# A limit of three loads in flight on SyncE in the listed opening phase of a retention and feed-forward kernel

## The chip, the cores and the metric

The kernel runs on one core of a Trainium2 chip. The metric is the device time of one execution in microseconds (us), lower is better. A difference of about 0.5% (4.4 us) is what the measurement can tell from no change.

## What is computed

Attention without softmax but with a decay by distance ("retention") over 4 batches, 8 heads, 576 positions and a head size of 64, then two feed-forward layers over the 2304 tokens of width 512:

```python
scores = scale * np.matmul(q, k.transpose(0, 1, 3, 2))
ret = scores * Dmat[None]            # Dmat[h, i, j] = gamma[h] ** (i - j), 0 above the diagonal
x = np.matmul(ret, v)                # reshaped to 2304 x 512
h = x @ w_in                         # 512 -> 2048
g = np.where(h >= 1, h, np.where(h <= -1, 0.0, (h + 1) ** 2 / 4))
x = g @ w_out                        # 2048 -> 512
out = ((x @ w_a) * (x @ w_b)) @ w_out2      # 512 -> 1536 -> 512
```

The weights are stored in double precision and are converted in the kernel.

## The kernel before

The tokens are cut into 18 chunks of 128 and 6 blocks of 384. For a chunk the retention needs a `u` tile of 1 MB (queries, keys, keys by row and values), which two loads of 512 KB bring (`load_chunk`, line 460; chunks 4 and 5 lie in tiles named `uw`). A weight tile is loaded as `raw`, 512 KB of doubles (`load_raw`, line 184), and then turned into a high and a low float32 part by ScalarE, VectorE and GpSimd.

The opening phase, some 113 us long, is written out by hand: `ORDER` (line 41) is a list of tokens, each a letter and a number, and every engine receives its instructions in the order of that list. The letters that matter here: `u` loads a chunk, `r` a raw weight tile, `c` a part of the constants; `S` multiplies queries by keys, `V` scales the values on GpSimd, `P` makes the chunk's output on TensorE (tiles `po`); `X`, `C`, `O` bring it to the tile `x`; `A`, `B`, `F` or `f`, `H`, `W` are the five steps of a weight tile's conversion (`A` on ScalarE waits for the raw tile's landing); `L` is a product of the first feed-forward layer (tile `ph`), `T`, `U`, `G`, `J` its activation, `Z` a product of the second (`acc`); `K` is filler work on TensorE (`idle`). All loads of this phase stand on SyncE's queue (SP), in the order of the list, and SP issues nothing else in it. `BANKS` gives the PSUM bank of every `S`, `P` and `L`; the list `planned` holds what is left of it, so it is empty from the last such token (`L12`, near the end of the list) on.

The framework gives each DMA one of eight landing semaphores in turn (`DMAHW0` to `DMAHW7`). A DMA that takes one over waits for the landing of the one that held it, so up to eight DMAs are in flight. After the listed phase the order is by loops and a scheduler; the change does not reach there.

Of the kernel before, what the change touches and what calls it, by code (L numbers as in the profile page):

```python
# [10 lines left out]
SYNC = mybir.DependencyInfo(mybir.DependencyClass.Sync, mybir.DependencyReason.DATA)  # L11
# [23 lines left out]
PACE = 1.2  # L35
MID = 288
CHUNKS = 4
SPARE, INTER_FIRST = (4, 5), 6
Q0, K0, R0, V0 = 0, 512, 0, 512

# [79 lines left out]
def retention_ffn_kernel(  # L120
# [12 lines left out]
    nc = tc.nc  # L133
    B, H, S, D = shape
    DM = H * D
# [14 lines left out]
    planned, ps = [int(n) for n in BANKS], []  # L150
# [26 lines left out]
    raw_pools, raw_turn, raw_every = [rpool], [0], [5]  # L177
    side = [nc.sync]

    def load_raw(src):  # L180
        r = raw_pools[-1] if raw_turn[0] % raw_every[0] == raw_every[0] - 1 else rpool
        raw_turn[0] += 1
        raw = r.tile([P, 512], I64, tag="raw", name="raw")
        side[0].dma_start(raw.rearrange("p (c f) -> p c f", f=src.shape[-1]), src)
        return raw

    def begin(raw, t=None):
# [63 lines left out]
    class Raws:  # L251
# [6 lines left out]
        def fetch_to(self, n):  # L258
            while self.begun < min(n, len(self.sources)):
                self.tiles[self.begun] = load_raw(self.sources[self.begun])  # L260
                self.begun += 1
# [139 lines left out]
    loads = []  # L401
# [18 lines left out]
    apool = att.enter_context(tc.tile_pool(name="att", bufs=1))  # L420
    upool = att.enter_context(tc.tile_pool(name="unit", bufs=CHUNKS))
    a2 = att.enter_context(tc.tile_pool(name="att2", bufs=2))
# [28 lines left out]
    def load_chunk(c):  # L451
        if c < NCH:
            if c in SPARE:
                two = [wpool.tile([P, 2, 512], F32R, tag="w", name="uw") for _ in range(2)]
                units[c] = [t.bitcast(F32).rearrange("p a c -> p (a c)") for t in two]
            else:
                t = upool.tile([P, 4 * DM], F32, tag="u", name="u")
                units[c] = [t[:, :2 * DM], t[:, 2 * DM:]]
            for part, t in enumerate(units[c]):
                nc.sync.dma_start(t, qkv[c, :, 2 * DM * part:2 * DM * part + 2 * DM])  # L460

    def prepare(c):

# [138 lines left out]
    def load_next(limit):  # L602

        while loaded[0] < min(limit, NCH):
            load_chunk(loaded[0])
            loaded[0] += 1
# [13 lines left out]
    def output_next():  # L620

        c = done[0]
        load_next(c + CHUNKS)
        given = output(c)
# [426 lines left out]
    def needed(step):  # L1051
# [1 line left out]

    half, parts, chunk, gen = {}, {}, {}, {}
    in_order = {
        "c": lambda k: nc.sync.dma_start(
            *((t[:, early:first] if k else t[:, :early]) for t in (con, const))
        ),
        "u": load_chunk, "r": lambda k: raws1.fetch_to(k + 1),
        "S": score, "V": prepare, "P": lambda c: chunk.update({c: evacuate(c, *output(c))}),  # L1060
        "X": lambda c: next(chunk[c]), "C": lambda c: next(chunk[c]), "O": lambda c: next(chunk[c]),
# [39 lines left out]
    for s, step in enumerate(steps[:last_by_hand]):  # L1101
        if s < by_order:
            continue
        i, b, f, first, last = step
# [49 lines left out]
    for s, step in enumerate(steps):  # L1154
        if s < last_by_hand:
            continue
        i, b, f, first, last = step
# [61 lines left out]
    for n in range(NSB):  # L1219
# [3 lines left out]
        for p in range(NF2 // 2):  # L1223
            for w in range(2):
# [11 lines left out]
                if quad:  # L1236
# [5 lines left out]
                    else:  # L1242
                        act2(other, quad)
                        f = 2 * quad.at[1]
# [73 lines left out]
```

## Time and profile before

| | |
|---|---|
| median of 3 runs | 874.16 us (873.89 to 878.53) |
| the profiled execution, its own time | 874.88 us |
| its span, first to last instruction | 873.0 us |
| TensorE matmul (PE) busy | 862.5 us, 99% |
| VectorE (DVE) busy | 577.4 us, 66% |
| ScalarE (ACT) busy | 446.5 us, 51% |
| GpSimd (POOL) busy | 81.1 us, 9% |
| DMA, mean over the span | 273 GB/s |
| DMA packets by queue | q1, loads and stores of SP: 196.87 MB; q0, of POOL: 40.37 MB; q8, instructions: 0.82 MB |

The profile is one execution. A row of the timeline tells start, duration, engine, line, operation, the tile written and the tiles read, how many instructions were merged, and in brackets how long the engine had been idle before and what ended that; "issue" there means that nothing the profile shows ended it. All products stand on line 157, a helper, so the tile's name tells them apart. The granted clock is the share of TensorE's full clock that the chip granted.

### The profile page before, as it was taken

The numbers are of one execution on the slowest core, as the hardware profiler recorded it, in microseconds if no ns is written. First come the engines' busy times: TensorE is split into PE (matmuls) and PEld (weight loads), VectorE is DVE, ScalarE is ACT, GpSimd is POOL, SyncE is SP. The second block draws the span as 40 slices with busy tenths as digits, with TensorE's granted clock in tenths as the row PEclk, the third lists the DMA queues.
The fourth block names the chain that finished last, engine by engine and source line by source line (L and its number), as shares of the span: only waits on it lengthen the run. The fifth ranks groups of instructions, "written<-read, shape, count | busy, mean of one in ns | idle before, by whom it ended". The sixth has DMA issues, their size and how long they took to land.

```text
span 873.0 us, 16378 instructions
## 1 busy us (share of the span) xinstructions
PE 862.5 (99%) x6308; PEld 847.7 (97%) x6308; DVE 577.4 (66%) x1088; ACT 446.5 (51%) x899; POOL 81.1 (9%) x124
## 2 busy tenths in 40 slices
PE   8899999999999999999999999999999999999998
PEld 6799999999999999999999999999999999999998
DVE  5787556576777789777779858752347575246465
ACT  4556355575766677666567546442233353333253
POOL 2313233110010011011001000000000000000000
PEclk9999999999999999999999999999999999999999
DMA  9997581648679889899889998879547589847583
GB/s 337 356 337 255 204 279 58 263 149 315 241 258 329 309 291 322 329 352 331 286 302 323 404 410 263 257 245 338 174 145 245 187 276 413 324 146 245 185 288 151
DMA packets 81373, 238.31 MB, mean 273 GB/s; under 512 B 8424, under 2 KB 35304, under 8 KB 78992
## 3 DMA queue, kind: packets, MB, share of 16 engines
q1 hardware_dynamic: 71616, 196.87, 63.2%
q0 software_dynamic: 9664, 40.37, 13.4%
q8 instruction: 50, 0.82, 0.4%
q14 instruction: 27, 0.22, 0.1%
q10 hardware_dynamic: 16, 0.02, 0.0%
HBM read 175.89 MB, written 61.34 MB: 272 GB/s over the span
## 4 chain that ended last, share of the span: by engine, by line
PE 99%; issue 1%; DVE 0%; ACT 0%
PE acc L157 35%; PE ph L157 23%; PE qx L157 17%; PE qy L157 9%; PE late L157 4%; PE qz L157 4%; PE po L157 4%; PE s L157 2%; PE idle L157 1%; PE wacc L157 0%; DVE keep L849 0%; DVE warm L1001 0%; ACT ost L976 0%
## 5 line engine op out<-in xcount | busy, mean ns | idle before, releaser
L157 PE MATMUL acc<-g,w 128*128 128x384 f32 x1296 | 249.0, 334 | 0.0
L157 PEld LDWEIGHTS acc<-g,w 128*128 128x128 f32 x1296 | 226.5, 188 | 0.4
L157 PE MATMUL ph<-x,w 128*128 128x384 f32 x1152 | 220.9, 336 | 0.0
L157 PEld LDWEIGHTS ph<-x,w 128*128 128x128 f32 x1152 | 201.6, 188 | 0.8 <-issue 0.2
L157 PE MATMUL qx<-tx,w 128*128 128x384 f32 x864 | 164.7, 334 | 0.0
L157 PEld LDWEIGHTS qx<-tx,w 128*128 128x128 f32 x864 | 151.1, 188 | 0.0
L793 ACT COPY keep<-qx 128x384 f32<-128x384 f32 x126 | 59.6, 480 | 141.3 <-PE qx L157 133.5
L661 ACT ACTIVATE t<-ph 128x384 f32<-128x384 f32 x96 | 47.1, 490 | 79.3 <-PE ph L157 75.1
L664 DVE SCALAR_TENSOR_TENSOR t<-t,ph 128x384 f32<-128x384 f32 x96 | 52.8, 551 | 51.9 <-ACT t L662 51.5
L157 PE MATMUL qy<-tx,w 128*128 128x384 f32 x432 | 86.3, 334 | 0.0
L157 PE MATMUL acc<-sp,w 128*128 128x384 f32 x432 | 77.5, 334 | 0.0
L157 PEld LDWEIGHTS qy<-tx,w 128*128 128x128 f32 x432 | 75.9, 188 | 0.0
L157 PEld LDWEIGHTS acc<-sp,w 128*128 128x128 f32 x432 | 75.1, 188 | 0.0
L669 ACT CAST g<-t 128x384 fp32r<-128x384 f32 x96 | 49.0, 510 | 40.7 <-DVE t L664 34.8
L671 DVE TENSOR_TENSOR g<-t,g 128x384 fp32r<-128x384 f32 x96 | 53.5, 557 | 20.8 <-ACT g L669 20.5
L886 DVE TENSOR_TENSOR sp<-gb,sp 128x768 fp32r<-128x768 f32 x42 | 40.1, 956 | 21.3 <-ACT sp L885 21.0
L662 ACT ACTIVATE t<-t 128x384 f32<-128x384 f32 x96 | 50.5, 526 | 2.7
L885 ACT CAST sp<-gb 128x768 fp32r<-128x768 f32 x42 | 35.1, 837 | 32.3 <-PE acc L157 18.8
L196 ACT ACTIVATE raw<-raw 128x512 int32<-128x512 uint32 x68 | 45.6, 671 | 2.7 <-DMA raw<-in_moe_w_out 2.7
L828 DVE TENSOR_TENSOR keep<-keep 128x384 f32<-128x384 f32 x36 | 20.0, 557 | 40.4 <-ACT keep L793 40.4
L157 PE MATMUL qz<-tx,w 128*128 128x384 f32 x216 | 43.4, 334 | 0.0
L815 DVE TENSOR_TENSOR keep<-qz,keep 128x384 f32<-128x384 f32 x36 | 20.0, 556 | 32.1 <-PE qz L157 27.7
(113 smaller groups left out, 944.9 us busy)
## 6 DMA issues: line engine op xcount, KB each, us to landing
w<-q SPq DMA_DIRECT2D x126, 512.0 KB, 5.3
q<-q SPq DMA_DIRECT2D x42, 512.0 KB, 7.1
w<-o SPq DMA_DIRECT2D x42, 512.0 KB, 5.1
x<-xd SPq DMA_DIRECT2D x12, 1536.0 KB, 8.6
u<-in_qkv SPq DMA_DIRECT2D x32, 512.0 KB, 8.3
raw<-in_moe_w_out POOLq DMA_DIRECT2D x18, 512.0 KB, 6.5
yin<-y SPq DMA_DIRECT2D x48, 192.0 KB, 4.3
xd<-x POOLq DMA_DIRECT2D x5, 1536.0 KB, 8.7
```

The lines of the kernel that those rows point to most:

```text
L157: return nc.tensor.matmul(o, l, r, start=start, stop=stop, skip_group_check=goes_on)
L196: nc.scalar.activation(r, low, AF.Copy, scale=2.0 ** -29)
L661: nc.scalar.activation(t, ph[:, :TB], AF.Relu, bias=0.5, scale=0.5)
L662: nc.scalar.activation(t, t, AF.Square)
L664: nc.vector.scalar_tensor_tensor(out=t, in0=t, scalar=1.0, in1=ph[:, :TB], op0=ALU.min, op1=ALU.max)
L669: hi = nc.scalar.copy(g[:, 0, :], t)
L671: anchor[:] = [hi, nc.vector.tensor_sub(g[:, 1, :], t, g[:, 0, :].bitcast(F32))]
L793: kept_by[0] = nc.scalar.copy(t, o[:, :HT])
L815: anchor[:] = [kept_by[0], nc.vector.tensor_add(self.c11, z[:, :HT], self.c11)]
L828: nc.vector.tensor_add(self.c22, self.c22, self.s5)
L885: nc.scalar.copy(t[:, 0], b)
L886: nc.vector.tensor_sub(t[:, 1], b, t[:, 0].bitcast(F32))
```

## The change

A constant `AHEAD = 3` and a function `load` are added. The loads of the phase go through it, and while `planned` is not empty each one gets a dependency on the landing of the third last.

```diff
+AHEAD = 3
...
+    sent = []
+
+    def load(to, of):
+        ins = side[0].dma_start(to, of)
+        if planned and len(sent) >= AHEAD:
+            tc.add_manual_dep(ins.ins, sent[-AHEAD].ins.name, SYNC, reason="loads in flight")
+        sent.append(ins)
+
     def load_raw(src):
...
-        side[0].dma_start(raw.rearrange("p (c f) -> p c f", f=src.shape[-1]), src)
+        load(raw.rearrange("p (c f) -> p c f", f=src.shape[-1]), src)
...
             for part, t in enumerate(units[c]):
-                nc.sync.dma_start(t, qkv[c, :, 2 * DM * part:2 * DM * part + 2 * DM])
+                load(t, qkv[c, :, 2 * DM * part:2 * DM * part + 2 * DM])
...
-        "c": lambda k: nc.sync.dma_start(
+        "c": lambda k: load(
```

Nothing changes its place on any engine; what changes is what the loads on SP wait for. Its queue from the second load of weights to chunk 5, before (`raw_330` and `raw_332` are raw weight tiles 1 and 2, `u_339` is chunk 3, the `uw` tiles are chunks 4 and 5; in brackets the semaphores waited for):

```order
L184 DMA raw_330<-in_moe_w_out 128x512 [waits DMAHW2_49]
L184 DMA raw_332<-in_moe_w_in 128x4x128 [waits DMAHW3_49]
L460 DMA u_339<-in_qkv 128x1024 [waits DMAHW4_49]
L460 DMA u_339<-in_qkv 128x1024 [waits DMAHW5_49]
L460 DMA uw_345<-in_qkv 128x1024 [waits DMAHW6_49]
L460 DMA uw_346<-in_qkv 128x1024 [waits DMAHW7_49]
L1056 DMA con_171<-in_const 128x192 [waits DMAHW0_49]
L460 DMA uw_485<-in_qkv 128x1024 [waits DMAHW1_49]
L460 DMA uw_486<-in_qkv 128x1024 [waits DMAHW2_49]
```

The same rows of SP now:

```order
L186 DMA raw_330<-in_moe_w_out 128x512 [waits DMAHW7_49,DMAHW2_49]
L186 DMA raw_332<-in_moe_w_in 128x4x128 [waits DMAHW0_49]
L186 DMA u_339<-in_qkv 128x1024 [waits DMAHW1_49]
L186 DMA u_339<-in_qkv 128x1024 [waits DMAHW2_49]
L186 DMA uw_345<-in_qkv 128x1024 [waits DMAHW3_49]
L186 DMA uw_346<-in_qkv 128x1024 [waits DMAHW4_49]
L186 DMA con_171<-in_const 128x192 [waits DMAHW5_49]
L186 DMA uw_485<-in_qkv 128x1024 [waits DMAHW6_49]
L186 DMA uw_486<-in_qkv 128x1024 [waits DMAHW7_49]
```

Each waits for the semaphore three places back in the turn of eight instead of its own one eight places back; the small load of constants counts as one of the three.

The end of the limit on SP, before (`u_1518` is chunk 14, `u_1602` chunk 15, `u_1835` chunk 16):

```order
L460 DMA u_1518<-in_qkv 128x1024 [waits DMAHW0_49,PE_49]
L460 DMA u_1518<-in_qkv 128x1024 [waits DMAHW1_49]
L460 DMA u_1602<-in_qkv 128x1024 [waits DMAHW2_49,PE_49,Pool_49]
L460 DMA u_1602<-in_qkv 128x1024 [waits DMAHW3_49]
L184 DMA raw_1748<-in_moe_w_in 128x4x128 [waits DMAHW4_49,DVE_49]
```

And now:

```order
L186 DMA u_1518<-in_qkv 128x1024 [waits DMAHW5_49,PE_49]
L186 DMA u_1518<-in_qkv 128x1024 [waits DMAHW6_49]
L186 DMA u_1602<-in_qkv 128x1024 [waits PE_49,Pool_49]
L186 DMA u_1602<-in_qkv 128x1024
L186 DMA raw_1748<-in_moe_w_in 128x4x128 [waits DVE_49]
```

From chunk 15 on no load waits for the third last one.

## Rows read from the trace of the kernel before

**Rows 1.** Busy time by stretch: us (instructions); last columns clock, DMA share, GB/s.

```profile
core 0: us, PE busy (x) PEld busy (x) DVE busy (x) ACT busy (x) POOL busy (x), PEclk, DMA share, GB/s
32.00:34.00 2.00, 2.00 (x21) 1.88 (x18) 1.45 (x4) 0.66 (x2) 0.00 (x0) 0.50 1.07 404
36.00:38.00 2.00, 2.00 (x51) 1.76 (x48) 1.14 (x4) 1.36 (x3) 1.78 (x3) 1.00 0.70 241
```

**Rows 2.** Chain of waits, 14 to 46 us: start, duration, what.

```profile
16.07 1.00 issue
...
21.56 0.57 PE s L157 x9
22.13 1.35 issue
...
26.39 0.83 PE s L157 x22
...
27.49 2.29 issue
29.78 2.65 PE po L157 x58
32.43 3.03 PE ph L157 x12
...
37.52 2.30 PE ph L157 x12
...
40.65 2.29 PE acc L157 x12
42.94 0.83 PE s L157 x22
```

**Rows 3.** Busy time between block starts at 17.05, 23.46, 29.76, 36.95, columns as before.

```profile
17.05:23.46 6.41, 5.06 (x126) 3.93 (x126) 5.51 (x13) 2.87 (x5) 1.13 (x2) 1.00 1.03 405
...
29.76:36.95 7.19, 7.17 (x122) 6.49 (x126) 4.05 (x9) 3.67 (x7) 1.86 (x4) 0.76 1.04 382
```

**Rows 4.** Queue 8 in windows 20.85:20.95 and 37.4:37.5: packets, MB, share.

```profile
q8 instruction: 1, 0.02, 68.2%
...
q8 instruction: 1, 0.02, 58.3%
```

**Rows 5.** Timeline of SP from 19 us: issues of loads.

```profile
20.05 0.33 SPq L184 DMA_DIRECT2D raw<-in_moe_w_out  x1
21.32 0.38 SPq L184 DMA_DIRECT2D raw<-in_moe_w_in  x1
```

**Rows 6.** DMAs issued at 10.25, 14.10, 20.05, 24.56: size, us to landing.

```profile
uw<-in_qkv SPq DMA_DIRECT2D x1, 512.0 KB, 11.1
...
uw<-in_qkv SPq DMA_DIRECT2D x1, 512.0 KB, 10.4
...
raw<-in_moe_w_out SPq DMA_DIRECT2D x1, 512.0 KB, 9.8
...
u<-in_qkv SPq DMA_DIRECT2D x1, 512.0 KB, 10.8
```

**Rows 7.** DMAs issued at 108.39, 70.66, 54.70, little else in flight: the same.

```profile
u<-in_qkv SPq DMA_DIRECT2D x1, 512.0 KB, 4.3
...
raw<-in_moe_w_out SPq DMA_DIRECT2D x1, 512.0 KB, 3.5
...
u<-in_qkv SPq DMA_DIRECT2D x1, 512.0 KB, 6.9
```

**Rows 8.** Timelines of ACT and DVE, from raw tile 3 to the first activation's end.

```profile
34.13 0.68 ACT L195 ACTIVATE conv<-raw 128x512 f32<-128x512 f32 x1
...
35.49 0.49 ACT L661 ACTIVATE t<-ph 128x384 f32<-128x384 f32 x1
...
38.26 0.55 DVE L671 TENSOR_TENSOR g<-t,g 128x384 fp32r<-128x384 f32 x1
```

## The prediction

> **What bounds the kernel now.** I read the page's chain first: 99% of the span is TensorE, so the end moves only where TensorE's own idle time or its clock moves. The chain of the opening phase shows that idle time: three pieces called "issue", 1.00, 1.35 and 2.29 us, ending at 17.07, 23.48 and 29.78 [rows 2]. Nothing the profile names ended them, and each lies in the middle of a row of equal products. The rows by block tell what they are: from one such restart to the next TensorE runs 126 products and 126 weight loads, 252 instructions [rows 3]; the page counts 12,616 of them in the kernel and 50 packets, 0.82 MB, on the instruction queue, which is 252 to a packet of 16 KB. So TensorE stands still because its next 16 KB of instructions are not there.
>
> When they come is seen in queue 8. After the block that starts at 17.05 its successor's packet starts near 20.9, 3.8 us later [rows 3, 4]; TensorE has used up its block at 22.13 and goes on at 23.48, some 2.6 us after the packet's start [rows 2]. The stretch has a DMA share of 1.03 [rows 3]: eight loads are queued. The block that starts at 36.95 has its packet at about 37.4, 0.5 us later [rows 3, 4], in a stretch whose DMA share has dropped to 0.70, the loads nearly drained [rows 1]. The start of a block in the profile is that of execution; the sequencer may be up to about 1 us ahead of it where TensorE is not starved, so I read 0.5 to 1.5 us for a short queue and 3.8 for a long one. After the third stall the granted clock is 0.50, the lower of its two levels (1.2 against 2.4 GHz), in 32 to 34 us [rows 1], so the next output and product take 2.65 and 3.03 us [rows 2]; a product at full clock takes 2.30 [rows 2].
>
> The loads themselves land one after another, 1.27 us apart in a full queue (each issue on SP at 20.05 and 21.32 follows a landing [rows 5]), and each in the order of its issue.
>
> **Part one: the instruction packets.** With three loads queued instead of eight, a packet should be in the state of 37 us, not of 17 us. A cycle from block to block is then 0.5 to 1.5 plus 2.6, that is 3.1 to 4.1 us, instead of 3.8 + 2.6 = 6.4. TensorE needs 5.06 and 4.01 us for these blocks (22.13 - 17.07 and 27.49 - 23.48 [rows 2]), so all three stalls go, or nearly. I take them as gone; if a packet still waits 3.8 us they all stay.
>
> The Trainium skill (DMA: Bandwidth & Descriptors, Queues, rings and completion order) has each DMA engine take turns between queues packet by packet. By that an instruction packet would wait for one turn, however long the load queue is, and this part would be worth nothing; 3.8 against 0.5 us speaks against it, but the two places differ in more than the queue. It is a rival below.
>
> **Part two: the loads.** Each now waits for the third last landing, and behind a waiting load stand only other loads on SP; nothing else is issued there in this phase. Waiters are `V` on GpSimd, `S` on TensorE, `A` on ScalarE. A wake-up on SP costs nothing I can see, and the change adds one semaphore instruction. The price is in whether three loads fill the queue: when load k lands, two are left, 2 x 1.27 = 2.5 us, and load k+3 lands no sooner than its own latency. Bounds for that latency: 3.5 us for a weight load and 4.3 us for a chunk's with little in flight, 6.9 for one right behind another [rows 7]. Three slots at 1.27 make 3.8 us, so 3.5 costs nothing, 4.3 stretches the spacing to 1.43, and 6.9 to 2.3. A gain I exclude: loads land in the order of their issue, so one that is held back frees nothing for one ahead of it. I take 4.3: most of these loads are of that kind, and the 6.9 holds a wait for the load in front.
>
> The Trainium skill (DMA: Bandwidth & Descriptors, Anatomy of one DMA) gives 2.0 us plus bytes over 436 GB/s, an estimate of 3.2 us for 512 KB. By that three would fill the queue and the loads would lose nothing; rows 7 are longer.
>
> At 1.43, 0.16 a load: the first loads land slowly anyway, so I count from chunk 2. Chunk 4's first half lands at 10.25 + 11.1 = 21.3 now [rows 6] and six loads on at 22.2. Chunk 5's first half, 14.10 + 10.4 = 24.5 [rows 6], loses 0.16 more and a whole slot less its own transfer, about 1.2, to the small load of constants, and with rounding lands at 27.0. Raw tile 3, 20.05 + 9.8 = 29.85 [rows 6], four loads later at 33.0. Chunk 7's first half, 24.56 + 10.8 = 35.4 [rows 6], four more at 39.2.
>
> **What TensorE then does.** S4 starts when chunk 4 is there. It starts at about 21.5 now, with the data at 21.3, so the first stall's removal is worth nothing here: 22.2, 0.7 later. The second stall, 1.35, is gone, so P3 begins 0.65 earlier. S5, at 26.39 now [rows 2], would be ready at 25.7 but waits for chunk 5: 27.05, again 0.7 late. The third stall is gone and P4 runs at full clock: S5 takes 0.83 and P4 about 1.9 (64 products; the chain's po rows at full clock have that), so it ends at 29.8, where the first product L0 stands at 32.43 now [rows 2]: 2.6 earlier. L0 at 2.30 instead of 3.03 makes 3.35. What is late next is the activation: on ScalarE it stands behind the conversion of raw tile 3 (34.13, then 35.49 [rows 8]), two steps of 0.68. They end at 33.0 + 1.4 = 34.4, not at L0's end of 32.1. From the activation's start to the split's end is 38.26 + 0.55 - 35.49 = 3.3 us [rows 8], so the second layer's product can start at 37.7; it starts at 40.65 now [rows 2]: 3.0 earlier. S7 (42.94 now [rows 2], 39.9 then) finds chunk 7 at 39.2. Later loads are issued when TensorE frees their buffers and shift with it, and the chain shows TensorE full from here on, so the 3.0 us stay to the end.
>
> **Sum**, against the profiled execution's own 874.88 (span 873.0 and 1.9 around it): 874.88 - 3.0 = 871.9. That execution lies 0.7 above the median of 874.16, which a comparison by medians takes off: 871.2.
>
> **The rivals.**
> *The loads lose nothing.* Latency at or below 3.8. Then S4 starts at 21.35, S5 at 24.7 (its chunk is there at 24.5), P4 ends at 27.4, L0 at 29.7, 5.8 us earlier than now, and raw tile 3 at 29.85 delays the activation to about 31.2, which its 1.8 us of slack before the second product takes up. 874.16 - 5.8 = 868.4; with half a microsecond lost at the start 868.9. For it: continuous flow hides the slow first packets of an idle queue that rows 7 hold. Against it: 2.5 us of queued work is short of every latency in rows 7.
>
> *The instruction packets come no sooner.* Then the stalls stay and the loads arrive within the time that TensorE stands still: 873.2 to 875, middle 874.2. This is the change not doing what it would have to, by the turn-taking above; against it stands the 0.5 us at 37.4.
>
> *The loads starve.* This one is slower. At a latency of 5.4 us, two fifths of the way from 4.3 to 6.9, spacing is 1.8. Chunk 7's first half is 17 slots on from chunk 2: 16 x 0.53 and 1.5 for the constants' slot are 10.0 us, so S7 waits until 45.4, 2.5 later than now, and the idle stretches bring the lower clock as after 29.78, 1.5 us (2.65 - 1.9 on the output and 3.03 - 2.30 on the product [rows 2]) that TensorE pays once now already and would pay once more; 874.2 + 2.5 + 1.5 = 878.2. It decides from about 4.9 us, where 16 x 0.37 and 1.4 make the 7.5 us that chunk 7 now lies ahead of S7. For it: the 6.9 of rows 7.
>
> A lower clock after the idle time before S5 would also cost the forecast 1.5 us: 872.7, inside its own range of 869.8 to 873.2.
>
> **How the numbers follow.** Forecast, 871.2: 0.52. Loads lose nothing, 868.6: 0.22. Packets no sooner, 874.2: 0.13. Starved, 876 to 881: 0.13. The predicted time is the likeliest's. Range: below, the second case's 868.4 less a little, 868.0; above, through the third case and the near half of the fourth, 877.0; about 0.06 is left out below and 0.08 above. The limit of 0.5%, about what a measurement of this kernel can tell from no change, is 4.4 us: faster means below 869.8, slower above 878.5. Faster: the second case almost whole and a little of the first, 0.24. Slower: the far half of the fourth, 0.08, and 0.02 for what I don't see, 0.10. Same: 0.66.
>
> **What the changed profile would show.** Packets of queue 8 starting 0.5 to 1.5 us after a block's start instead of 3.8; no "issue" pieces inside rows of equal products between 14 and 30 us; instead TensorE idle ahead of S4 and S5, ended by a DMA. The time to landing of the chunk loads 4 to 5 us instead of 10 to 11, and landings 1.27 to 1.43 apart. Granted clock 1.00 in 30 to 34 us. The second layer's first product at 37 to 38 us. The prediction is wrong if the three pieces are still there, if landings are over 1.6 us apart, or if the gain is given back between 45 us and the end.

## The result, and the profile after

| | before | changed |
|---|---|---|
| median, 7 runs each | 874.26 us (873.89 to 878.53) | 879.28 us (878.60 to 881.65) |
| ratio, 95% interval | | 1.0053 [1.0033, 1.0072], about 0.5% slower |
| profiled execution, its own time | 874.88 us | 879.28 us |
| its span | 873.0 us | 877.4 us |

A ratio, here and below, is not quite that of the two medians, and it leaves out three runs in a slow state (one of the kernel before at 1422 us, one with six loads in flight at 1061, one with five at 3011).

The forecast was 871.2 us in a range of 868.0 to 877.0. The time lies above the range, on the other side of no change, and by about as much as the measurement can tell from no change; the rival that came true is "the loads starve", which had a chance of 0.13 and a price of 878.2 us.

The work on TensorE is the same: one row of the changed kernel's page, its busy time and instructions, and the row of the chain's shares by engine.

```profile
PE 861.7 (98%) x6308; PEld 847.0 (97%) x6308; DVE 578.7 (66%) x1088; ACT 446.8 (51%) x899; POOL 81.2 (9%) x124
...
PE 92%; DMA 8%; issue 0%; DVE 0%; ACT 0%; SPq 0%
```

The chain used to be 99% TensorE; now 8% of the span are DMAs. Where they lie is seen in the chain of the changed kernel, 14 to 50 us (start, duration, what), which answers to [rows 2]:

```profile
8.62 5.47 DMA u<-in_qkv
...
14.12 5.07 DMA raw<-in_moe_w_in
...
19.20 5.24 DMA uw<-in_qkv
...
24.46 4.59 DMA uw<-in_qkv
...
29.07 5.08 DMA u<-in_qkv
...
34.16 5.27 DMA raw<-in_moe_w_out
...
39.44 6.85 DMA u<-in_qkv
```

This is the limit itself: each of these loads is the third one after the row above it, and starts 0.02 us after that one has landed. From 8.62 to the last landing at 46.29 seven turns of three loads take 37.67 us, 1.79 us a load. In the full queue it was 1.27 [rows 5].

The same in the windows of 17 to 30 us (us, busy times and counts, clock, DMA share, GB/s), first of the kernel before, then of the changed one, which also has the stretch after 45 us:

```profile
17.00:30.00 13.00, 9.30 (x263) 7.60 (x262) 10.46 (x23) 4.90 (x12) 2.79 (x6) 1.00 1.03 400
```

```profile
17.00:30.00 13.00, 8.08 (x248) 6.64 (x248) 10.04 (x21) 5.76 (x13) 3.48 (x7) 1.00 0.79 260
...
45.16:49.40 4.24, 4.24 (x97) 3.71 (x97) 3.27 (x5) 1.52 (x3) 1.54 (x2) 0.60 0.99 412
```

The DMA engines were full and are now 0.79 busy. TensorE's clock, 0.50 at 32 to 34 us in [rows 1], is now 1.00 there and falls later: it has a mean of 0.60 from 45.16 to 49.40, where the lower of the two levels is granted from 45.88 to 49.30.

TensorE's timeline in the changed kernel (start, duration, tile, count, and in brackets the idle time before and what ended it):

```profile
14.23 0.90 PE L158 MATMUL s<-u 64*64 64x64 f32 x32 [1.37 <-DMA u<-in_qkv]
...
20.93 0.67 PE L158 MATMUL po<-u,state 64*64 64x128 f32 x16 [1.64 <-DVE state L606]
...
24.58 0.90 PE L158 MATMUL s<-uw 64*64 64x64 f32 x32 [1.64 <-DMA uw<-in_qkv]
...
29.18 0.90 PE L158 MATMUL s<-uw 64*64 64x64 f32 x32 [1.36 <-DMA uw<-in_qkv]
...
31.72 2.36 PE L158 MATMUL ph<-x,w 128*128 128x384 f32 x12
...
40.69 2.38 PE L158 MATMUL acc<-g,w 128*128 128x384 f32 x12
45.16 0.94 PE L158 MATMUL s<-u 64*64 64x64 f32 x32 [2.09 <-DMA u<-in_qkv]
...
67.49 0.90 PE L158 MATMUL s<-u 64*64 64x64 f32 x32 [0.49 <-DMA u<-in_qkv]
```

No idle time is left that nothing ended: the three "issue" pieces of [rows 2] are gone. In their place stand waits for loads: for chunk 2 (14.23, S2), chunk 4 (24.58, S4), chunk 5 (29.18, S5), chunk 7 (45.16, S7) and one at 67.49; the output at 20.93 waits for VectorE, whose state update stands behind the conversion of raw tile 1. Set against the same instructions of the kernel before, TensorE is 0.7 us late at S2, 3.1 late at S4, 2.9 late at S5, 0.6 early at the first product (31.72 against 32.36), level at the second layer's product (40.69 against 40.59), 2.3 late at S7, 3.8 late behind the low clock, and 4.3 late from 67.5 on; to the end of the span it stays 4.3 to 4.4. (Starts are those of the timeline; the chain's pieces in [rows 2] start up to 0.07 later.)

### The profile page after: what moved, and what is told of

Read it like the earlier page. It is cut to its first block, busy times and chain, and to the rows that moved or that the text cites. A ratio compares the mean times of both kernels' runs of the same rounds, so it can differ in the third digit from the quotient of the medians.

```text
span 877.4 us, 16379 instructions
## 1 busy us (share of the span) xinstructions
PE 861.7 (98%) x6308; PEld 847.0 (97%) x6308; DVE 578.7 (66%) x1088; ACT 446.8 (51%) x899; POOL 81.2 (9%) x124
## 4 chain that ended last, share of the span: by engine, by line
PE 92%; DMA 8%; issue 0%; DVE 0%; ACT 0%; SPq 0%
PE acc L158 34%; PE ph L158 21%; PE qx L158 17%; PE qy L158 9%; PE late L158 4%; PE qz L158 4%; DMA u<-in_qkv 3%; PE po L158 2%; DMA raw<-in_moe_w_out 2%; DMA raw<-in_moe_w_in 1%; DMA uw<-in_qkv 1%; PE s L158 1%; DMA con<-in_const 0%; DVE keep L860 0%; ACT ost L987 0%
```

## Experiments

All numbers in flight below are set by the constant or the condition of the one new function; nothing else differs from the changed kernel. A kernel "with four" lets four loads be in flight. Medians are of 10 to 12 runs, except where the number is given. The kernel before was run beside each group, with medians of 874.3 to 875.1 us, so differences between kernels of two groups are good to about 1 us; the ratios, each to the kernel before of its own group, allow for that. A trace is that of one execution.

**Two and four.** If three are too few because of a load's own latency, the time must turn sharply between two, three and four.

```diff
-AHEAD = 3
+AHEAD = 2
```

> Two loads in flight. Theory: a load's own latency is about 4.5 us with one in front, so one lands in 2.2 to 2.6 us; over the 24 loads to chunk 8 that is some 20 us later than with three: 895 to 905 us, TensorE idle ahead of most of the listed phase's products for a DMA. Instruction packets start 0.5 to 1.5 us after a block's start. Rival one (a fixed price a load): 879 to 881 us.

One run: 897.73 us. Its waits of TensorE between 10 and 70 us (us in total, times, longest), then its window from 8 to 39 us:

```profile
PE s L158 <- DMA u<-in_qkv: 13.0, 4, 8.1
PE s L158 <- DMA uw<-in_qkv: 4.8, 2, 2.6
```

```profile
8.00:39.00 31.00, 19.90 (x425) 15.34 (x421) 15.77 (x33) 10.03 (x21) 6.23 (x10) 0.82 0.68 219
```

The median of its loads from issue to landing is 4.6 us between 9 and 39 us, against 5.2 with three. Two slots of 1.27 are 2.5 us, little over half of that latency, and the DMA share is 0.68. A fixed price for each waiting load would not have done this: the same loads wait in both kernels.

```diff
-AHEAD = 3
+AHEAD = 4
```

> The limit is four loads in flight instead of three. Theory (a load issued behind others takes at least about 5.2 us to land, as the changed kernel's chunk loads do, so n in flight land one in 5.2/n us, but never under the 1.27 us of a full queue; and instruction packets come sooner in a shorter queue): 5.2/4 = 1.30, so the loads lose about 1 us by chunk 7 and TensorE is no longer held by them; of the instruction stalls of before (1.00, 1.35, 2.29 us) a part goes: 871.5 to 874.5 us. Rival one (every load that waits pays a fixed price of its own, whatever the depth): as slow as the limit of three, 878 to 880 us. Rival two (instruction packets do not care for the queue): the stalls and the packets' 3.8 us after a block's start are as before, 874 to 875.5 us.

873.09 us, ratio to the kernel before 0.9979 [0.9964, 0.9994]: one load more in flight takes 6.2 us off the changed kernel, back to the kernel before or a little under it (the interval ends just below 1). The waits of TensorE in it, 10 to 70 us, and two rows of its chain:

```profile
PE po L158 <- issue: 1.9, 3, 1.0
PE po L158 <- DVE state L606: 1.4, 1, 1.4
PE s L158 <- DVE ret L508: 0.6, 1, 0.6
PE s L158 <- DMA uw<-in_qkv: 0.3, 1, 0.3
```

```profile
30.32 2.29 PE ph L158 x12
...
38.43 2.29 PE acc L158 x12
```

Little waiting for loads is left: 0.3 us for chunk 5, and at most the 0.6 us of S4 in the third row, where chunk 4's first half lands at 22.76, just when VectorE's `ret` ends. Three "issue" pieces remain, 1.9 us in all instead of 4.6. The first product starts 2.1 us before that of [rows 2] and runs at full clock, the second layer's at 38.43 stands 2.2 earlier, and these 2.2 us stay to the end (span 870.8 against 873.0). The loads are late here too: chunk 4's first half lands at 22.8, chunk 5's at 26.3, raw tile 3 at 33.0 and chunk 7's first half at 39.05. TensorE does not come to S7 before 40.65, so S7 does not wait. The DMA engines are not quite full with four either, in the window 17 to 30 us:

```profile
17.00:30.00 13.00, 9.71 (x291) 8.06 (x295) 11.11 (x24) 6.42 (x14) 3.87 (x8) 1.00 0.90 296
```

The median from issue to landing is 6.6 us, more than four slots (5.1). What four leave of lateness, 3.65 us at chunk 7 (39.05 against 35.40), lies within the 7.5 us that chunk 7 was ahead of S7.

**Five and six.**

```diff
-AHEAD = 3
+AHEAD = 5
```

> Five loads in flight. Theory: 5.2/5 = 1.04 is under 1.27, the loads lose nothing; the instruction packets gain little or nothing over before: 873 to 874.5 us. Rival one: 877 to 880 us. Rival two: 874 to 874.5 us with stalls of 1.0, 1.35 and 2.3 us.

873.72 us, ratio 0.9981 [0.9965, 0.9997]; of this kernel only the times are used.

```diff
-AHEAD = 3
+AHEAD = 6
```

> Six loads in flight. Theory: nothing lost, nothing gained, 874 to 874.5 us, stalls as before. Rival one: still 877 or more.

873.83 us, ratio 0.9985 [0.9971, 1.0000]. Rows of its chain:

```profile
26.37 2.18 issue
28.55 2.98 PE po L158 x58
31.53 2.67 PE ph L158 x12
```

The third "issue" piece is back, 2.18 against 2.29 us, and the low clock behind it. From four to six the gain in the medians shrinks only from 1.7 to 0.9 us, and the intervals overlap: the medians do not tell four from six. The two traces do differ, in the third piece and in the clock.

What the instruction packets did, worked out from the traces (start of every 252nd instruction of TensorE and of the next packet on queue 8, three blocks; the row with two begins one block earlier than the others; the last column is the difference):

```
in flight   block starts           its packet starts      us later
two         11.60  21.39  31.77    13.13  21.60  32.76    1.53  0.21  0.99
three       16.44  24.87  29.93    17.45  27.22  33.38    1.01  2.35  3.45
four        16.30  23.19  28.41    19.51  26.13  32.51    3.21  2.95  4.10
six         16.10  22.35  28.55    20.01  26.11  32.38    3.91  3.76  3.84
eight       17.07  23.48  29.77    20.90  27.29  33.63    3.83  3.81  3.86
```

Only the middle block is clear: its packet comes 3.8 us after it with six and eight in flight and 2.1 to 3.3 after it in every trace with three or four of these loads, the kernels further below included. It is the packet that ends the third piece: with four it comes 0.9 us sooner, which makes up most of the 1.3 us by which that piece shrinks. The other two blocks do not follow the number in flight: with three the first has 1.0 here, but 4.3 in the kernel with the limit up to chunk 5, and the third has 3.3 to 4.1 at every number from three to eight. With two and three in flight TensorE also stands waiting for data, and its sequencer may then enter a block before the block's first instruction starts (with two, the packet at 64.42 starts some 0.3 us before its block), so the short delays are not clean.

**A load of 1 MB as one.** If it is bytes behind the limit that lack, and not the number of loads, three larger loads are enough. All chunks but 4 and 5 are brought by one DMA each.

```diff
+            if c not in SPARE:
+                load(t, qkv[c])
+                return
             for part, t in enumerate(units[c]):
```

(`SPARE` are chunks 4 and 5, which keep their two halves.)

> Limit of three as in the changed kernel, but a chunk (except 4 and 5) is brought by one DMA of 1 MB instead of two of 512 KB. Theory (a load's latency is some 4 us plus its own transfer, so what starves the queue is too few bytes behind the limit): one 1 MB load takes about 6.5 us, three of mixed size hold 5 to 7.5 us of transfer, the queue stays full, the loads land as in the kernel before, 872.5 to 875 us; instruction packets come as late as with five or six loads of the small size, 3 to 3.8 us after a block's start. Rival (the number of loads decides, each costs its turn): landings in the same slots as with three small ones, fewer slots by a third in this stretch but each twice as long, 877 to 880 us.

875.50 us, ratio 1.0005 [0.9993, 1.0017]: half a microsecond above the first expectation and 1.5 below the rival's, 3.8 us better than the changed kernel, with the same three in flight, though not as good as four. TensorE at S7 in its timeline:

```profile
42.33 1.51 PE L158 MATMUL s<-u 64*64 64x64 f32 x32 [4.55 <-DMA u<-in_qkv]
```

Until then TensorE was 5.2 us ahead of the kernel before, the most of all these kernels; the "issue" pieces are down to 0.32 to 0.41 us. But chunk 7, issued as one at 32.77, lands at 42.19 only, behind weights and, from 38.8 us on, together with a store of 1.5 MB, and S7 gives all but 0.5 us of it back; the lower clock follows (42.44 to 45.85). So up to 40 us three larger loads do as well as a longer queue, which speaks for the bytes in flight and against a price for each load; what a large load costs here is the landing of the one that is wanted next.

**Which stretch costs it.** Four kernels place the limit by the number of loads already sent (the 15th and 16th behind the first are chunk 5's halves, the 19th is raw tile 3, the 23rd and 24th chunk 7's).

```diff
-        if planned and len(sent) >= AHEAD:
+        if AHEAD <= len(sent) <= 16:
```

> The limit of three only as far as chunk 5's second half, none (eight) from chunk 6 on. Theory: S5 starts as late as in the changed kernel, 2.9 us behind the kernel before, and the instruction stalls up to there are gone; from then on loads land 1.3 us apart, chunk 7 at about 40 to 41 instead of 45 to 46.3 us, so S7 no longer waits long and the clock does not fall after it: 872 to 874.5 us. Rival (the loss lies in the first stretch): 878 to 880 us.

876.60 us, ratio 1.0016 [1.0006, 1.0026]: between the two expectations, and 2.7 us better than the changed kernel. Its timeline at S4 and its windows:

```profile
25.89 0.90 PE L158 MATMUL s<-uw 64*64 64x64 f32 x32 [2.31 <-DMA uw<-in_qkv]
```

```profile
24.00:30.00 6.00, 4.11 (x100) 3.62 (x104) 3.53 (x6) 0.00 (x0) 2.87 (x5) 0.77 0.69 226
30.00:36.00 6.00, 6.00 (x112) 5.52 (x111) 5.43 (x11) 2.94 (x8) 1.13 (x2) 0.66 0.95 342
```

The limit up to chunk 5 costs the wait before S4 all the same. Behind it the clock falls, at 27.25 already, so that TensorE comes to S5 (30.45) after chunk 5 has landed; 1.5 us of lateness at the second layer's product stay to the end. S7 no longer waits.

```diff
-AHEAD = 3
+AHEAD = 4
...
-        if planned and len(sent) >= AHEAD:
+        if planned and len(sent) >= 15:
```

> No limit (eight) as far as the constants, then a limit of four. Theory: S4 and S5 start as in the kernel before or earlier, the third stall of 2.29 us shrinks to about 1 us as with four throughout, and the clock stays at its upper level after it: 870.5 to 872.5 us, 1 to 2 us better than four throughout. Rival (the packets of this stretch were asked for while the queue was still long, and come no sooner): 873 to 874.5 us.

872.98 us, ratio 0.9984 [0.9969, 0.9999], between the two expectations. Timeline:

```profile
27.43 1.06 PE L158 MATMUL po<-ret,uw 64*64 64x64 f32 x26 [1.08 <-issue]
```

In its profiled execution TensorE is 3.7 us ahead of the kernel before at S7, the clock never falls, and an "issue" piece of 1.08 us is what is left of 2.29. Over the kernel with four throughout nothing can be told apart by the medians.

```diff
-        if planned and len(sent) >= AHEAD:
+        if planned and len(sent) >= 15:
```

> No load waits for an earlier one until the constants; from chunk 5 on each waits for the third last landing. It is the same as the kernel with four from chunk 5 on (872.98 us), but three. By the theory (with three in flight a load lands some 1.75 us after the one ahead of it, with four 1.3): the stretch up to 24 us is that of the kernel before, chunk 5's first half lands near 25 us, chunk 7's eight loads later near 25 + 8 x 1.75 + 1.5 for the stores of xd = 40.5 us, where S7 would start at 39 in the run with four; so S7 waits about 1.5 us, and with a lower clock behind it 1.5 to 3.8 more: 874.0 to 877.5. Rival: three in flight are enough once the opening rush is over, and all of the loss comes from the first stretch: 872.5 to 873.5, as with four.

875.60 us, ratio 1.0013 [0.9999, 1.0027]: 2.6 us slower than the same kernel with four, so three are too few after the opening rush as well. S7 in its timeline:

```profile
42.35 0.90 PE L158 MATMUL s<-u 64*64 64x64 f32 x32 [1.84 <-DVE w L235]
```

The row names VectorE, but chunk 7's first half, issued at 35.48, lands at 42.22 (6.74 us), 0.13 before the start, as the loads do before S4, S5 and S7 of the changed kernel (0.13 to 0.14). The wait is put down to the load. TensorE was 2.4 us ahead of the kernel before at 38 us and 0.5 ahead after this wait; from there to 64 us it lost another 1.5, 1.0 of it in one wait for GpSimd at 62.40. The clock did not fall.

```diff
+        far = AHEAD if len(sent) < 19 else 4
         if planned and len(sent) >= AHEAD:
-            tc.add_manual_dep(ins.ins, sent[-AHEAD].ins.name, SYNC, reason="loads in flight")
+            tc.add_manual_dep(ins.ins, sent[-far].ins.name, SYNC, reason="loads in flight")
```

> Three in flight up to chunk 6, four from raw tile 3 on (19 loads stand ahead of it). By the theory S4 and S5 wait as in the changed kernel and the first product of the first layer starts near 31.7 us, but from raw tile 3 on a load lands 1.3 us after the one ahead of it and not 1.75: raw tile 3 a little before 36.6 us, chunk 7's first half near 42.5 instead of 45.0. S7 then waits at most 0.5 us, no lower clock follows, and nearly the whole of the 4.3 us is saved: 874 to 876. Rival: what is lost before 30 us stays lost, the late chunk 7 is only where it shows: 877 to 879.5.

875.67 us, ratio 1.0013 [1.0003, 1.0023]. Its timeline at S4 and S7, and the window after:

```profile
25.92 0.90 PE L158 MATMUL s<-uw 64*64 64x64 f32 x32 [2.38 <-DVE x L609]
...
43.14 0.90 PE L158 MATMUL s<-u 64*64 64x64 f32 x32
```

```profile
42.00:48.00 6.00, 6.00 (x115) 5.44 (x115) 5.56 (x12) 4.00 (x8) 3.26 (x4) 1.00 0.97 387
```

S4 and S5 start later even than in the changed kernel (25.92 and 29.67; the row at S4 names VectorE, but chunk 4's first half lands at 25.78, 0.14 before it), and the first product starts 0.6 us late. But chunk 7's first half lands at 42.16 and not at 45.02, S7 starts without a wait, the clock stays, and 3.6 of the changed kernel's 5.0 us are saved. This settles the second half of the loss: it is the late chunk 7 and what follows it, and it is not there with four in flight from raw tile 3 on.

**The constants.** The small load of constants takes one of the three places. Without a place of its own it should cost nothing.

```diff
-        "c": lambda k: load(
+        "c": lambda k: (nc.sync.dma_start if k else load)(
```

> As the changed kernel, but the 96 KB load of constants is outside the limit. Theory: its slot costs about 1.2 us of every later landing, so chunk 5 lands near 27.9 instead of 29.05 us and chunk 7's second half near 45 instead of 46.3; S5 and S7 wait that much less: 877.5 to 878.5 us. Rival (the slot is not what is short, the latency is hidden there): no change, 879 to 879.5 us.

878.88 us in four runs, ratio 1.0045 [1.0033, 1.0058]. The time lies between the two expectations and within the interval of the changed kernel, and the trace differs by more than the edit. Its windows:

```profile
24.00:30.00 6.00, 4.14 (x85) 3.76 (x88) 3.64 (x7) 0.25 (x1) 2.73 (x5) 0.61 0.88 298
30.00:36.00 6.00, 6.00 (x121) 5.14 (x122) 4.38 (x8) 2.44 (x7) 1.13 (x2) 0.54 0.79 266
```

In this execution the clock is at its lower level for most of 24 to 36 us, S5 starts at 31.65, later than in the changed kernel, and S7 waits only 0.15 us. Chunk 5 lands at 29.83, no earlier than with the constants under the limit (29.05). What the constants' place costs stays open.

## Why the prediction was wrong, point by point

**The bound and the stalls.** That TensorE stood still for its instructions holds: with eight or six in flight the third piece is 2.29 and 2.18 us, with four 1.00, with three none, and 0.2 and 0.5 in two other kernels that have three there. The size of the step was not right. I took 0.5 to 1.5 us from a block's start to its packet for three in flight; the changed kernel shows 1.0 to 3.5. That all three pieces went is in part owed to TensorE waiting for loads in the same blocks, which gave the packets time. That the middle block's packet comes at 2.95 us with four and 3.8 with six and eight speaks against a wait of one turn only, as the prediction took it from the Trainium skill (DMA: Bandwidth & Descriptors, Queues, rings and completion order), but weakly: the other two blocks do not show it. What sets the delay stays open.

**The loads: the step that failed.** I chose 4.3 us for a load's latency with two others in front, out of 3.5, 4.3 and 6.9 [rows 7], and so a spacing of 1.43. The changed kernel's loads issued from 9 to 39 us have a median of 5.2 (those whose landing the trace shows). The groups of issues at 10.30, 31.43 and 38.23 us (size, us to landing) answer to [rows 6]:

```profile
u<-in_qkv SPq DMA_DIRECT2D x1, 512.0 KB, 6.3
...
raw<-in_moe_w_out SPq DMA_DIRECT2D x1, 512.0 KB, 5.2
...
u<-in_qkv SPq DMA_DIRECT2D x1, 512.0 KB, 6.8
```

The 5.2 is over the deciding point of 4.9 that the prediction itself gave (16 x 0.37 and 1.4 are 7.3 and not its 7.5, which moves the point to 4.95), and a third of it is 1.73, against the 1.79 us a load measured above and the 1.6 that the prediction named as a sign of being wrong. The estimate of 3.2 us that the prediction worked out from the Trainium skill (DMA: Bandwidth & Descriptors, Anatomy of one DMA) is further off; 5.2 with two in front is 2.0 over it, and the section gives that sum for DMAs issued by GpSimd, where these are issued by SyncE. The lateness against the kernel before, as forecast and as measured:

```
                          forecast   measured   landed, before and now
chunk 2, second half         0         2.5      14.08   16.58
chunk 4, first half          0.9       3.1      21.30   24.44
chunk 5, first half          2.5       4.6      24.48   29.05
raw tile 3                   3.2       6.8      29.85   36.64
chunk 7, first half          3.8       9.6      35.40   45.02
```

Two terms make the difference. The start, which I counted at nothing up to chunk 2 because the first loads land slowly anyway, costs 2.5: the kernel before had seven loads queued at 5 us and eight from 8 us on. And the loads behind chunk 5 lose more than the 0.16 that I had: the four up to raw tile 3 lose 0.55 each, the next two nothing, and the two to chunk 7's first half 2.8 together.

Between chunk 2 and chunk 4 (0.13 a load) and at the constants (1.4) this execution agrees with the forecast, but that is chance. In the traces of the three other kernels that have the same limit up to there (up to chunk 5, three and then four, the constants free), chunk 4's first half lands at 25.8 to 25.9 and not at 24.44, a loss of 0.4 to 0.5 a load, and the step at the constants is 0.5 to 0.75, no smaller where the constants are free. All four agree on chunk 5: 4.6 to 5.4 us late.

Where the last 2.8 come from is not settled. It is not the 1.5 MB store of `xd` alone: up to 43.45 all packets are those of SP's loads. The windows of the changed kernel before and after that, columns as above:

```profile
41.00:43.45 2.45, 2.07 (x12) 1.75 (x10) 2.42 (x6) 1.77 (x5) 1.50 (x2) 1.00 0.78 157
43.45:45.05 1.60, 0.00 (x0) 0.00 (x0) 0.95 (x2) 1.60 (x4) 0.80 (x1) 1.00 0.96 387
```

Before the store the engines move 157 GB/s; with the full queue, in 17 to 30 us, it was 400.

The landings that I forecast for three are those of four: chunk 4 at 22.2 (four: 22.8), chunk 5 at 27.0 (26.3), raw tile 3 at 33.0 (33.0), chunk 7 at 39.2 (39.05). The time is still 873.09 us and not 871.2, with 1.9 us of the instruction stalls left.

**TensorE.** From S5 to the first product the step held: 6.04 us before [rows 2], 2.54 now, a gain of 3.5 where 3.3 was forecast; but S5 was 2.9 late and not 0.7, so only 0.6 of it was left. The activation stood behind raw tile 3's conversion, as said. On ScalarE in the changed kernel, answering to [rows 8]:

```profile
36.72 0.67 ACT L206 ACTIVATE conv<-raw 128x512 f32<-128x512 f32 x1 [3.13 <-DMA raw<-in_moe_w_out]
37.29 0.66 ACT L207 ACTIVATE raw<-raw 128x512 int32<-128x512 uint32 x1
37.85 0.48 ACT L672 ACTIVATE t<-ph 128x384 f32<-128x384 f32 x1
```

The mechanism was right and its start 3.6 us late: the second layer's product came at 40.69 instead of 37.7. The last step, S7 not waiting, was wrong: chunk 7's lateness in the table above became the 2.09 us in front of S7.

**The sum.** Level at the second layer's product; then 2.2 at S7, 1.5 in the low clock behind it (2.3 late before, 3.8 after), 0.6 at 67.49. That is the 4.3 us, against the −3.0 of the forecast: of the 7.3 between them, 3.0 were lost before the second layer's product and the rest behind it.

**The rivals.** "The loads starve" told the mechanism, its place and nearly its size: S7 at 45.4 (45.16), a lower clock after it for 1.5 us (1.5), at a latency of 5.4 (5.2). It left out the 0.6 us at 67.49. That its S7 comes so close is in part luck: it too counted the start at nothing, where 2.5 us were lost, and had 10.0 us for the loads from chunk 2 to chunk 7, where the changed kernel lost 7.1. Its chance of 0.13 was too low for a case whose deciding point, 4.9, lay between two of the three rows on which the choice stood: the load with another right in front of it, 6.9, was nearer to a load with two in front than the lone ones that I took. "The loads lose nothing" fell, and so did "packets come no sooner": the stalls went and the time left its range.

**Open.** Why the clock falls where it does. It falls behind a wait of 2.09 us here, 2.18 with six, 2.31 with the limit up to chunk 5 and 4.55 with joined loads, but not behind 1.84 us with three from chunk 5 on, nor behind 2.38 us with three and then four. So the 1.5 us of the sum are read from this execution, and no run here tells what decides them.

## What to carry to other kernels

A limit of n loads in flight spaces them by their latency at that depth over n, wherever that is longer than one load's transfer (here 2.28 us with two, at a latency of 4.6, and 1.79 with three, at 5.2, against 1.27 in a full queue); so measure the latency behind other loads, not that of a lone one. Add up the lateness along the queue to the tile whose slack is smallest against it, from the first load on, and compare it with that slack before counting what the shorter queue gives elsewhere. When the choice between a few rows of a trace decides the sign, the chance belongs to both sides of it.

## What was not expected of the hardware

The packet with TensorE's next 252 instructions starts 3.8 us after its block in all three blocks with six or eight loads of 512 KB queued; with four it is 3.2, 2.95 and 4.1, and the third stall shrinks from 2.3 and 2.2 to 1.0 us with the middle one. A load of 512 KB takes 4.6 us with one other in flight, 5.2 with two and 6.6 with three, against 3.5 and 4.3 alone [rows 7]: even four loads, 2 MB, did not keep the DMA engines full. And chunk 7's first half took 6.8 us, and 6.7 with three from chunk 5 on, where the median is 5.2. The 1.5 MB store from GpSimd shares the DMA engines only for the last 1.5 to 2.0 us of these two loads; what part of it is the store's was not tried. A load that lies beside the whole store does take long: with two in flight chunk 7's first half takes 9.7 us (51.83 to 61.51, the store's packets from 52.86 to 60.58), where the median is 4.6, and it is the longest wait of that kernel, 8.1.
